# Second MoE by seven products: where its operands are prepared, and which 4 KB tile each step takes

## The chip, the cores and the metric

The kernel runs on one core of a Trainium2 chip. The metric is the device time of one execution in microseconds (us). Its engines are named as the profile names them: PE (TensorE, matrix products), PEld (its weight loads), DVE (VectorE), ACT (ScalarE), POOL (GpSimd) and SP (SyncE, which here issues every DMA).

## What is computed

A softmax attention without a score matrix feeds a gated MoE and then a second MoE. All weights come as float64, and the result is float32.

```python
def _attn_ref(q, k, v):                    # each (8, 8, 576, 64)
    q_s = softmax of q over the last axis
    k_s = softmax of k over the 576 positions
    kv = np.einsum('bhsd,bhse->bhde', k_s, v)
    return np.einsum('bhsd,bhde->bhse', q_s, kv)

def _moe_ref(x, w_gate, w_val, w_out):     # x (4608, 512), d_ff 1536
    g = x @ w_gate
    silu = g * (1.0 / (1.0 + np.exp(-g)))
    return silu * (x @ w_val) @ w_out

def _moe2_ref(x, w_in, w_out):             # d_ff 2048
    h = x @ w_in
    g = np.where(h > 0.0, h, np.exp(np.minimum(h, 0.0)) - 1.0)
    return g @ w_out
```

(The two softmaxes are written out in the reference; here they are abridged.)

## The kernel before

The 4608 tokens are nine blocks of 512, numbered 0 to 8. Every matrix product is done three times with operands split into a high and a low part (high by high, high by low, low by high), so one product of two 128-wide operands is three PE instructions.

**First MoE, two passes.** `run_1` goes over the nine blocks twice: pass "a" with the first six chunks of d_ff (the attention of the next block is computed beside it, `side_1a`), pass "b" with the other six. A block of a pass is six chunks of three slots: slot 0 is the gate product and its silu on ACT (`silu_act`, L798 to L801), slot 1 the value product and silu's products on DVE (L805, L808, L811), slot 2 the product with `w_out` of the chunk before (`emit_B`) and the low half of the new `g` (L789). Each slot holds 12 matmuls, so a block has 216. The gate lies in one of two PSUM banks (`a0`, `a1`); PE may start the next gate only when L808 has read the last one. At a block's end four DVE adds (L845) form the block's result `ys`, which goes to DRAM.

**Weights.** `conv`, called in slots of both passes, turns float64 weights into the split form: a load into a `raw` tile (L142, L144), a scaling on ACT, three bit operations on DVE (L171 to L178), a split on ACT and POOL (L201, L202, L217 to L231), and a store to DRAM (`sd` for the second MoE's input weights, `wd` for its output weights).

**Operands of the second MoE.** It computes blocks in pairs by seven products (M1 to M7) of sums of quarter blocks. Its operands, `xd`, are made from `ys` by `prep_open` and `prep_step`: the first loads four tiles of one half (c = 0 or 1) of a pair into the tile `yr` (L935), the second makes one operand per call. That is a difference of quarters on DVE where one is wanted (L917), a copy on ACT that rounds to the high part (L959), one call later the low part on DVE (L949) and a store of 512 KB (L950). The operands go round three buffers of the staging tile `xst`, so the copy of the fourth waits until the store of the first has landed. `side_b` decides when: in blocks 2 to 7 of pass b one half each, opened in slot 3 and stepped from slot 6 on; in block 8 both halves of the last pair (blocks 6 and 7), two steps per slot. Block 8 has no partner; its operands are made in `x_one`, in the second MoE (L910, L917).

**Second MoE.** `run_2` goes over four pairs and the single block 8 with the first half of d_ff (half 0), then over them in reverse order with the other half (half 1). One unit is four steps (two for the single block) of `step`: the seven products, four exponential units (`elu_act`, `elu_stt`, `elu_max`, `elu_hi`, `elu_lo`) on ACT and DVE, and between them, as `mid`, the products with `w_out2` of the step before (`emit_D`, 24 matmuls per step and block). A unit's last step goes through `after`: the loads of the next unit's operands are issued (`x_big`, `x_small`: one tile of M1 and M6, six of M7, M5 and M2, one of M3 and M4), then comes the last `emit_D` of the first block with its evacuation (`evac`, L1085 to L1088), then `rest` (the fourth exponential unit), then the sums of the second block, whose last part is carried into the next unit's first step.

**Order and tiles.** The order on every engine is the order in which the code is written (`manual_schedule`), and all DMAs stand in one queue, SP's. Tiles of 4 KB a partition come from three pools, `w` (19), `raw` (3) and `g` (3), by `slot4`, which takes the first pool in a given order that has room.

## Time and profile before

| | |
|---|---|
| time, median of 3 runs | 1827.46 us (1827.08 to 1829.01) |
| time of the profiled execution | 1828.21 us |
| its span, first to last instruction | 1826.3 us |
| mean granted TensorE clock, share of full speed | 0.974 |
| busy: PE, PEld, DVE, ACT, POOL | 1713.7, 1399.4, 1147.1, 873.2, 164.3 us |
| moved by DMA | 317.32 MB, mean 174 GB/s |

The span is what the profile sees; 1.9 us of the execution lie around it. Busy time is the union of an engine's instructions; a matmul's end is modelled, so neighbours overlap a little. Line numbers (L...) are those of the kernel before. In a row on a stretch stand its start and end, its length, the busy time of PE, PEld, DVE, ACT and POOL (with the instructions in brackets), the granted clock as a share of full speed, the busy share of the DMA engines and GB/s.

### The profile page before, as it was taken

Reading aid. Unit: us, or ns where it says so; the run is one execution under the profiler, and the core shown is the slowest. Engines: PE = TensorE matmul, PEld = TensorE weight load, DVE = VectorE, ACT = ScalarE, POOL = GpSimd, SP = SyncE. Lnnn points to the kernel's source line nnn. Section 1 sums busy time; section 2 is a strip of 40 time slices with the busy share of each in tenths; the row PEclk is TensorE's granted clock in tenths of the full one; section 3 lists DMA queues with packets and bytes.
Section 4 is the critical chain, followed back from the end, with each engine's and each line's share of the span. In section 5 each row is a group of like instructions: output and inputs, shape, how many; then the busy total and the mean of one; then the engine's idle time right before and its main releaser. Section 6 shows DMA issues by size and latency. Waiting matters only on the chain.

```text
span 1826.3 us, 21717 instructions
## 1 busy us (share of the span) xinstructions
PE 1713.7 (94%) x8264; PEld 1399.4 (77%) x8264; DVE 1147.1 (63%) x1763; ACT 873.2 (48%) x1534; POOL 164.3 (9%) x140
## 2 busy tenths in 40 slices
PE   6799999999999979899997699999979889999999
PEld 4677888888788867677885578888869768888887
DVE  7867777775686666677553474746564447475574
ACT  5555444444464545455442364645453436354453
POOL 3620000000031434111000000000000000000000
PEclk9899999999999999999998799999989989999999
DMA  9374576543554786777557833314014713341511
GB/s 277 111 205 131 147 185 160 169 127 120 177 189 143 281 311 243 269 292 286 208 196 295 321 133 149 139 70 184 24 46 177 305 48 129 125 185 69 208 46 70
DMA packets 148360, 317.32 MB, mean 174 GB/s; under 512 B 46240, under 2 KB 97440, under 8 KB 134944
## 3 DMA queue, kind: packets, MB, share of 16 engines
q1 hardware_dynamic: 148256, 315.93, 50.1%
q8 instruction: 65, 1.06, 0.2%
q14 instruction: 39, 0.32, 0.1%
HBM read 200.54 MB, written 115.35 MB: 173 GB/s over the span
## 4 chain that ended last, share of the span: by engine, by line
PE 78%; DVE 8%; DMA 7%; ACT 5%; issue 1%; POOL 1%; SPq 1%; DVEq 0%; ACTq 0%; POOLq 0%
PE p L997 17%; PE y L753 11%; PE y L751 11%; PE y L752 10%; PE a L770 9%; PE a L771 9%; PE a L774 9%; DMA xd<-xst 3%; DMA yr<-ys 2%; PE t L431 1%; PE t L590 1%; DVE u L1121 1%; ACT th L1010 1%; ACT e L1011 1%; DVE g L1045 1%
## 5 line engine op out<-in xcount | busy, mean ns | idle before, releaser
L770 PE MATMUL a<-x,w 128*128 128x512 f32 x856 | 343.4, 401 | 57.6 <-DVE th L808 57.4
L771 PE MATMUL a<-x,w 128*128 128x512 f32 x856 | 338.5, 395 | 0.7 <-POOL x L599 0.7
L751 PE MATMUL y<-w,g 128*128 128x512 f32 x576 | 227.7, 395 | 20.8 <-ACT g L1036 11.5
L770 PEld LDWEIGHTS a<-x,w 128*128 128x128 f32 x856 | 163.9, 191 | 103.2 <-DVE th L808 56.8
L774 PE MATMUL a<-x,w 128*128 128x512 f32 x856 | 232.0, 393 | 0.0
L753 PE MATMUL y<-w,g 128*128 128x512 f32 x576 | 227.7, 395 | 0.8
L752 PE MATMUL y<-w,g 128*128 128x512 f32 x576 | 226.8, 394 | 0.0
L1121 DVE TENSOR_TENSOR u<-u,p 128x512 f32<-128x512 f32 x180 | 123.4, 686 | 139.7 <-PE p L997 131.8
L771 PEld LDWEIGHTS a<-x,w 128*128 128x128 f32 x856 | 164.1, 192 | 34.5 <-POOL x L599 1.2
L774 PEld LDWEIGHTS a<-x,w 128*128 128x128 f32 x856 | 163.1, 191 | 34.6
L997 PE MATMUL p<-xp,s 128*128 128x512 f32 x768 | 182.3, 391 | 3.9 <-DVE u L1121 3.9
L783 ACT ACTIVATE g<-th 128x512 fp32r<-128x512 f32 x108 | 68.3, 632 | 241.6 <-DVE th L811 241.6
L805 DVE SCALAR_TENSOR_TENSOR th<-th,e 128x512 f32<-128x512 f32 x108 | 77.5, 717 | 159.7 <-ACT th L801 159.7
L752 PE MATMUL y<-g,w 128*128 128x512 f32 x432 | 169.7, 393 | 2.4 <-POOL g L789 2.4
L753 PE MATMUL y<-g,w 128*128 128x512 f32 x432 | 170.0, 394 | 1.5 <-POOL w L202 1.5
L997 PEld LDWEIGHTS p<-xp,s 128*128 128x128 f32 x768 | 144.6, 189 | 34.8 <-DVE u L1121 4.8
L751 PE MATMUL y<-g,w 128*128 128x512 f32 x432 | 170.1, 394 | 1.2 <-ACT w L201 1.2
L1016 DVE SCALAR_TENSOR_TENSOR th<-e,th 128x512 f32<-128x512 f32 x144 | 99.3, 690 | 100.7 <-ACT e L1011 99.1
L997 PE MATMUL p<-xs,s 128*128 128x512 f32 (+1 forms) x720 | 154.6, 369 | 0.4 <-DVE u L1121 0.4
L751 PEld LDWEIGHTS y<-w,g 128*128 128x128 f32 x576 | 110.0, 191 | 44.8 <-ACT g L1036 12.4
L997 PEld LDWEIGHTS p<-xs,s 128*128 128x128 f32 x720 | 126.4, 189 | 23.4 <-DVE u L1121 0.6
L798 ACT ACTIVATE e<-a 128x512 f32<-128x512 f32 x107 | 63.8, 597 | 168.0 <-PE a L774 167.9
(179 smaller groups left out, 2532.0 us busy)
## 6 DMA issues: line engine op xcount, KB each, us to landing
xp<-xd SPq DMA_DIRECT2D x32, 1024.0 KB, 7.8
xd<-xst SPq DMA_DIRECT2D x56, 512.0 KB, 5.7
xs<-xd SPq DMA_DIRECT2D x48, 512.0 KB, 10.8
xs<-x SPq DMA_DIRECT2D x9, 2048.0 KB, 7.0
x<-xs SPq DMA_DIRECT2D x36, 512.0 KB, 8.0
sd<-s SPq DMA_DIRECT2D x8, 1792.0 KB, 6.8
s<-sd SPq DMA_DIRECT2D x8, 1792.0 KB, 14.0
raw<-in_moe_w_out SPq DMA_DIRECT2D x26, 512.0 KB, 4.9
```

Of the source, the lines that this page charges most:

```text
L751: nc.tensor.matmul(out=ps, lhsT=wh, rhs=xh, start=first, stop=False)
L752: nc.tensor.matmul(out=ps, lhsT=wh, rhs=xl, start=False, stop=False)
L753: nc.tensor.matmul(out=ps, lhsT=wl, rhs=xh, start=False, stop=last)
L770: nc.tensor.matmul(out=ps, lhsT=wh, rhs=x[:, c, 0, :], start=(c == 0), stop=False)
L771: nc.tensor.matmul(out=ps, lhsT=wh, rhs=x[:, c, 1, :], start=False, stop=False)
L774: nc.tensor.matmul(out=ps, lhsT=wl, rhs=x[:, c, 0, :], start=False, stop=(c == KD - 1))
L783: nc.scalar.activation(out=gt[:, 0, :], in_=src, func=ACTF.Copy)
L798: nc.scalar.activation(out=e, in_=gate, func=ACTF.Relu, scale=-1.0)
L805: nc.vector.scalar_tensor_tensor(out=t, in0=t, scalar=1.0, in1=e, op0=ALU.add, op1=ALU.mult)
L997: nc.tensor.matmul(out=out_, lhsT=w, rhs=x, start=first and (q, c, k) == (0, 0, 0), stop=(c, k) == (1, 2), skip_group_check=True,)
L1016: nc.vector.scalar_tensor_tensor(out=t, in0=e, scalar=1.0, in1=t, op0=ALU.add, op1=ALU.mult)
L1121: nc.vector.tensor_tensor(o, a, b, op=ALU.add)
```

## The change

The first two pieces of the diff give the kernel charge of the 4 KB tiles: 25 of them in one pool, each with its own name, a list of vacant ones, and `slot4` takes the one that has been vacant longest among the kinds it is given. `g`, `raw` and `w` tiles of the first MoE go through it too. In `side_b`, blocks 5, 6 and 7 of pass b now hold six openings, one every nine slots, for both halves of pairs 0, 1 and 2; blocks 2 to 4 and block 8 hold none. The halves of pair 3 and the single block are prepared by `prep_window`, behind `rest` of the pairs 0, 1 and 2 in half 0; `x_one` only loads. Two of four loads of input weights and four of eight of output weights for half 0 move from the end of block 8 into the first two steps of `run_2`. The single block's last sums are carried into the next unit, as a pair's were.

```diff
-    CAP = {"w": NW1, "raw": NRAW, "g": 3}
-    used = dict.fromkeys(CAP, 0)
+    KINDS = ("w",) * NW1 + ("raw",) * NRAW + ("g",) * 3
+    vacant = list(range(len(KINDS)))
+    ANY = ("w", "raw", "g")
...
+    def slot4(kinds, shape, name, dtype=F32R):
+        for n in vacant:
+            if KINDS[n] in kinds:
+                vacant.remove(n)
+                return n, wp.tile(shape, dtype, tag=f"m{n}", name=name)
         raise AssertionError(name)
 
-    def drop(tag):
-        used[tag] -= 1
+    def drop(n):
+        vacant.append(n)
...
+    PREP0 = 5
...
+    def prep_now(m, c, ops, outs):
+        lo = []
+
+        def finish():
+            op, src, d = lo.pop()
+            nc.vector.tensor_tensor(d[1], src, d[0].bitcast(FP32), op=ALU.subtract)
             for n in range(2):
+                nc.sync.dma_start(out=xd[m][PROD[op]][:, c, n], in_=d[n].bitcast(FP32))
+
+        for op, src, pre in ops:
+            d = outs.pop(0)
+            outs.append(d)
+            pre()
+            nc.scalar.activation(out=d[0], in_=src, func=ACTF.Copy)
+            if lo:
+                finish()
+            lo.append((op, src, d))
+        finish()
+
+    def prep_window(n):
+        m, single = (NB // 2 - 1, False) if n < 2 else (NB // 2, True)
+        at = [slot4(ANY, [128, 2, TB], "yr") for _ in range(3)]
+        r = [t[:, e].bitcast(FP32) for _, t in at[:2] for e in range(2)]
...
+        for t, (b, c) in zip(r, src):
+            nc.sync.dma_start(out=t, in_=ys[b][:, c])
...
+        if single:
+            outs = [(t[:, 0:256], t[:, 256:]) for t in (at[2][1][:, 0], at[2][1][:, 1], st[:, 0], st[:, 1], *cd)]
+            for c in range(2):
+                t = cg()
+                prep_now(m, c, prep_ops(
+                    r[2 * c][:, 0:256], r[2 * c][:, 256:], r[2 * c + 1][:, 0:256],
+                    r[2 * c + 1][:, 256:], t[:, 0:256], t[:, 256:],
+                ), outs)
+        else:
+            outs = [(at[2][1][:, 0], at[2][1][:, 1]), (st[:, 0], st[:, 1]), cd[0:2], cd[2:4]]
+            prep_now(m, n, prep_ops(*r, cg(), cg()), outs)
+        for t, _ in at:
+            drop(t)
...
     def side_b(i, ff, s):
...
+        n = (i - PREP0) * 3 * HALF + 3 * ff + s
+        if n < 0 or n > 6 * 9:
+            return
+        if n % 9 != 1:
+            prep_step()
+        if n % 9 == 0 and n < 6 * 9:
+            assert not prep
+            prep_open(n // 18, n // 9 % 2)
...
         if s == 2 and ff >= 1:
-            while len(wtag) < F2 // 2 and used["w"] < NW1:
-                load_p(len(wtag))
+            while len(wtag) < 4 and room(("w",)):
+                load_p(len(wtag), ("w",))
         if (ff, s) == (HALF - 1, 2):
-            assert not prep
             x_big(units[0], X_LAST)
-            load_s(2)
-            load_s(3)
...
             for k, q in enumerate(gs[:-1]):
+                if n == 0 and k < 2:
+                    load_s(2 + k)
+                    load_p(4 + 2 * k)
+                    load_p(5 + 2 * k)
...
                 if len(u) == 1:
                     rest()
-                dd(u[0], k, drop_w=turn)()
-                if len(u) == 2:
+                    carry.append(lambda a=(half, u[0], fs[k], turn): emit_D(*a))
+                else:
+                    dd(u[0], k)()
                     rest()
+                    if n < 3:
+                        prep_window(n)
```

Three places in the built order show what moves. The first is SP's queue in block 5 of pass b, from the load of the next block's input on. Before:

```order
L1252 DMA x<-xs_148 128x1024 x4
L950 DMA xd_185<-xst 128x1024
L204 DMA wd_119<-w 128x1024
L144 DMA raw<-in_moe_w_out 128x512
L950 DMA xd_188<-xst 128x1024
L853 DMA ev<-yp_156 128x2048
L950 DMA xd_186<-xst 128x1024
L950 DMA xd_189<-xst 128x1024
L204 DMA wd_120<-w 128x1024
L950 DMA xd_187<-xst 128x1024
L950 DMA xd_191<-xst 128x1024
```

and with the change (`yr<-ys` are the loads of the next half):

```order
L1277 DMA x<-xs_142 128x1024 x4
L984 DMA xd_176<-xst 128x1024
L984 DMA xd_174<-xst 128x1024
L208 DMA wd_113<-w 128x1024
L147 DMA raw<-in_moe_w_out 128x512
L984 DMA xd_178<-xst 128x1024
L862 DMA ev<-yp_150 128x2048
L984 DMA xd_177<-xst 128x1024
L969 DMA yr<-ys_154 128x512
L969 DMA yr<-ys_155 128x512
L969 DMA yr<-ys_154 128x512
L969 DMA yr<-ys_155 128x512
```

Before, seven stores `xd<-xst` of one half stand in this block; with the change the seven of one half are followed at once by the loads and stores of the next, in the same queue as the weight traffic (`wd`, `raw`), the next block's input (`x<-xs`) and the partial sums (`ev<-yp`).

The second is DVE where the first pair of the second MoE hands over to the second (`ev<-y` is the evacuation, `u<-u,p` the next step's first sums). Before:

```order
L1087 COPY ev<-y_8499 128x512
L1087 COPY ev<-y_8501 128x512
L1016 SCALAR_TENSOR_TENSOR th<-e,th 128x512
L1022 TENSOR_TENSOR th<-th,u 128x512
L1045 TENSOR_TENSOR g_8861<-th,g_8861 128x512
L1121 TENSOR_TENSOR u<-u,p_8947 128x512
L1121 TENSOR_TENSOR u<-u,p_8954 128x512
```

and with the change:

```order
L1073 TENSOR_TENSOR g_8800<-th,g_8800 128x512
L951 TENSOR_TENSOR u<-yr 128x512
L951 TENSOR_TENSOR u<-yr,u 128x512
L910 TENSOR_TENSOR yr<-yr 128x512
L910 TENSOR_TENSOR st<-u,st 128x512
L910 TENSOR_TENSOR xo<-yr,xo 128x512
L951 TENSOR_TENSOR yr<-yr,u 128x512
L910 TENSOR_TENSOR xo<-u,xo 128x512
L910 TENSOR_TENSOR yr<-yr 128x512
L951 TENSOR_TENSOR yr<-yr 128x512
L910 TENSOR_TENSOR st<-yr,st 128x512
L910 TENSOR_TENSOR xo<-yr,xo 128x512
```

Between the low part of `rest` (the last row of the `g` kind) and the next unit's sums stand eleven operations on what `ys` gives, and ACT has seven copies at the same place.

The third is PE where the single block passes from half 0 to half 1 (`p<-xa,s` and `p<-xs,s` are products, `y<-w,g` the sums with the output weights). Before, the products of half 1 follow the last sum:

```order
L751 MATMUL y_11086<-w_8215,g_11165 128x512
L752 MATMUL y_11086<-w_8215,g_11165 128x512
L753 MATMUL y_11086<-w_8215,g_11165 128x512
L997 MATMUL p_11252<-xa,s 128x256 x12
L997 MATMUL p_11265<-xa,s 128x256 x12
L997 MATMUL p_11278<-xa,s 128x256 x12
L997 MATMUL p_11296<-xa,s 128x256 x12
L997 MATMUL p_11252<-xs,s 128x256 x12
```

With the change the first five of these products stand ahead of the second half of the sums:

```order
L759 MATMUL y_11156<-w_8113,g_11004 128x512
L760 MATMUL y_11156<-w_8113,g_11004 128x512
L761 MATMUL y_11156<-w_8113,g_11004 128x512
L1025 MATMUL p_11260<-xa,s 128x256 x12
L1025 MATMUL p_11273<-xa,s 128x256 x12
L1025 MATMUL p_11286<-xa,s 128x256 x12
L1025 MATMUL p_11304<-xa,s 128x256 x12
L1025 MATMUL p_11260<-xs,s 128x256 x12
L759 MATMUL y_11153<-w_8272,g_11220 128x512
L760 MATMUL y_11153<-w_8272,g_11220 128x512
L761 MATMUL y_11153<-w_8272,g_11220 128x512
```

The 48 matmuls of the carried sums now follow the fifth product instead of standing ahead of the first. The same move is made where the single block hands over to pair 3 in half 1.

## Rows read from the trace of the kernel before

**Rows 1.** The page: TensorE's busy time, and its granted clock in 40 slices.
```profile
PE 1713.7 (94%) x8264; PEld 1399.4 (77%) x8264; DVE 1147.1 (63%) x1763; ACT 873.2 (48%) x1534; POOL 164.3 (9%) x140
PEclk9899999999999999999998799999989989999999
```

**Rows 2.** Waits of PE: who waited for whom, us in all, times, longest.
```profile
PE a L770 <- DVE th L808: 57.4, 11, 20.8
PE y L751 <- ACT g L1036: 11.5, 2, 5.8
PE y L751 <- DVE ev L1087: 9.3, 1, 9.3
```

**Rows 3.** Stretches of pass b, cut where L845 starts.
```profile
591.80:640.83 49.03, 49.03 (x218) 40.58 (x217) 32.22 (x47) 25.23 (x45) 23.07 (x21) 1.00 0.73 263
640.83:703.87 63.04, 52.30 (x217) 42.12 (x216) 40.55 (x59) 29.10 (x52) 22.14 (x21) 0.92 0.77 279
703.87:765.51 61.64, 51.55 (x216) 41.50 (x215) 39.99 (x58) 28.90 (x52) 15.90 (x13) 0.94 0.76 282
765.51:817.20 51.69, 49.26 (x217) 40.46 (x217) 37.61 (x58) 26.80 (x49) 8.29 (x6) 1.00 0.82 295
817.20:868.35 51.15, 49.26 (x217) 40.47 (x217) 38.64 (x58) 26.23 (x48) 7.79 (x6) 1.00 0.71 267
917.31:966.27 48.96, 48.96 (x217) 40.54 (x217) 25.48 (x41) 20.31 (x37) 0.00 (x0) 1.00 0.50 183
966.27:1048.79 82.52, 55.49 (x219) 44.45 (x219) 32.81 (x52) 23.98 (x43) 0.00 (x0) 0.81 0.88 334
```

**Rows 4.** Line L845: shortest, median, longest ns; first and last start.
```profile
L845 DVE TENSOR_TENSOR ev<-y,ev x36: 681/681/692, 591.8 to 1050.8; 128x512 f32<-128x512 f32 x36
```

**Rows 5.** Chain of waits, blocks 2 and 8: start us, us, what.
```profile
648.96 8.17 DMA yr<-ys
669.46 11.73 DMA xd<-xst
...
988.62 16.36 DMA xd<-xst
1013.36 10.92 DMA yr<-ys
```

**Rows 6.** Stretches of the second MoE, cut where a unit's first product starts.
```profile
1041.10:1122.04 80.94, 79.50 (x350) 65.17 (x348) 50.74 (x77) 42.32 (x71) 0.00 (x0) 1.00 0.48 189
1122.04:1204.04 82.00, 81.90 (x362) 67.51 (x360) 47.61 (x72) 42.67 (x72) 0.00 (x0) 1.00 0.30 116
1286.04:1380.22 94.18, 84.81 (x361) 69.36 (x360) 55.36 (x94) 47.50 (x86) 0.00 (x0) 0.95 0.09 34
1380.22:1489.46 109.24, 95.00 (x553) 84.14 (x552) 50.87 (x91) 44.73 (x88) 0.00 (x0) 0.94 0.51 202
1489.46:1570.50 81.04, 78.35 (x337) 64.07 (x336) 48.45 (x74) 40.47 (x68) 0.00 (x0) 0.98 0.38 143
```

**Rows 7.** Stretches: products with 256 columns; all DMA engines busy.
```profile
1392.90:1405.80 12.90, 12.90 (x109) 12.90 (x108) 8.82 (x17) 8.29 (x17) 0.00 (x0) 1.00 0.80 310
1090.00:1108.00 18.00, 17.91 (x80) 14.47 (x79) 12.35 (x19) 11.02 (x20) 0.00 (x0) 1.00 1.00 398
```

**Rows 8.** Timeline of ACT, blocks 7 and 5: start, us; idle in brackets.
```profile
946.35 0.64 ACT L959 ACTIVATE xst<-yr 128x512 fp32r<-128x512 f32 x1 [2.60 <-DMA xd<-xst]
848.72 0.63 ACT L959 ACTIVATE xst<-yr 128x512 fp32r<-128x512 f32 x1 [1.94 <-DMA xd<-xst]
```

**Rows 9.** The first pairs' turn, timeline of SP and ACT.
```profile
1088.66 3.57 SPq L872 DMA_DIRECT2D xs<-xd  x6
1106.54 0.32 SPq L1088 DMA_DIRECT2D y<-ev  x1
1123.60 0.60 ACT L1140 ACTIVATE u<-p 128x512 f32<-128x512 f32 x1 [13.11 <-PE p L997]
```

**Rows 10.** The four stores of the output's last block, as DMA issues.
```profile
out<-ev SPq DMA_DIRECT2D x4, 256.0 KB, 2.4
```

More of the change, by code (lines that the diff above doesn't have):

```diff
@@ L97, with room @@
         chunks.append((("p", f), wsrc_rows(w_out2, f), False))
-    CAP = {"w": NW1, "raw": NRAW, "g": 3}
-    used = dict.fromkeys(CAP, 0)
-    def slot4(order, shape, name):
-        for tag in order:
-            if used[tag] < CAP[tag]:
-                used[tag] += 1
-                pool = {"w": wp, "raw": raw_p, "g": g_p}[tag]
-                return tag, pool.tile(shape, F32R, tag=tag, name=name, bufs=CAP[tag])
+    KINDS = ("w",) * NW1 + ("raw",) * NRAW + ("g",) * 3
+    vacant = list(range(len(KINDS)))
+    ANY = ("w", "raw", "g")
+    def room(kinds):
+        return sum(KINDS[n] in kinds for n in vacant)
+    def slot4(kinds, shape, name, dtype=F32R):
[3 more added lines that the diff above has]
+                return n, wp.tile(shape, dtype, tag=f"m{n}", name=name)
         raise AssertionError(name)
-    def drop(tag):
-        used[tag] -= 1
+    def drop(n):
+        vacant.append(n)
     sd = [dr.tile([128, 7, 2, 256], FP32, name=f"sd{g}") for g in range(2 * NG2)]
@@ L139, in conv_load @@
         _, src, cols = chunks[n]
-        t = early.pop(n) if n in early else raw_p.tile([128, 512], I64, tag="raw", name="raw")
+        t = early.pop(n) if n in early else None
+        if t is None:
+            rslot[n], t = slot4(("raw",), [128, 512], "raw", I64)
         if cols:
@@ L194, in conv_split @@
             return
-        if used["w"] >= NW1:
+        if not room(("w",)):
             return
-        used["w"] += 1
-        w = wp.tile([128, 2, 512], F32R, tag="w", name="w", bufs=NW1)
+        at, w = slot4(("w",), [128, 2, 512], "w")
         stage["split"] += 1
@@ L533 @@
     xd = [
-        {op: dr.tile([128, 2, 2, TB], FP32, name=f"xd{t}{op}") for op in range(7)}
-        for t in range(NB // 2)
+        {
+            op: dr.tile([128, 2, 2, TB if t < NB // 2 else TB // 2], FP32, name=f"xd{t}{op}")
+            for op in range(7)
+        }
+        for t in range(NB // 2 + 1)
     ]
@@ L876, in x_small @@
                 o[op] = [t[:, c] for c in range(2)]
+                nc.sync.dma_start(out=t.bitcast(FP32), in_=xd[u[0] // 2][PROD[op]])
     def x_big(u, ops):
@@ new lines, in prep_window @@
+    def prep_window(n):
+        m, single = (NB // 2 - 1, False) if n < 2 else (NB // 2, True)
+        at = [slot4(ANY, [128, 2, TB], "yr") for _ in range(3)]
+        r = [t[:, e].bitcast(FP32) for _, t in at[:2] for e in range(2)]
+        src = [(2 * m, n), (2 * m + 1, n), (2 * m, n + 2), (2 * m + 1, n + 2)]
+        if single:
+            src = [(2 * m, 0), (2 * m, 2), (2 * m, 1), (2 * m, 3)]
+        for t, (b, c) in zip(r, src):
+            nc.sync.dma_start(out=t, in_=ys[b][:, c])
+        st = cv_p.tile([128, 4, 256], F32R, tag="st", name="st", bufs=1)
+        st = st.rearrange("p (a b) n -> p a (b n)", a=2)
+        cd = [cv_p.tile([128, TB], F32R, tag="cd", name="xo", bufs=NCD) for _ in range(4)]
+        if single:
+            outs = [(t[:, 0:256], t[:, 256:]) for t in (at[2][1][:, 0], at[2][1][:, 1], st[:, 0], st[:, 1], *cd)]
[10 more added lines that the diff above has]
+            drop(t)
@@ L1027, in g_tile @@
         if key not in G2:
-            G2[key] = slot4(("g", "w", "raw"), [128, 2, TB], "g2")
+            G2[key] = slot4(ANY, [128, 2, TB], "g2")
         return G2[key][1]
@@ L1421, in run_2 @@
                     x_big(nxt, X_HEAD)
-                    x_small(nxt, X_MID, ("raw", "w", "g"))
+                    x_small(nxt, X_MID, ANY)
             k = len(gs) - 1
@@ L1439, in after @@
                             x_big(nxt, X_HEAD)
-                            x_small(nxt, X_MID, ("raw", "w", "g"))
+                            x_small(nxt, X_MID, ANY)
                     if len(nxt) == 2:
```

63 lines of the change are left out of this document (16 added, 47 removed).

## Prediction

> **What bounds the kernel now.** PE is busy for 1713.7 of 1826.3 us [rows 1], so only its idle time, and what it does at the lower of its two clock levels, can be saved. The granted clock's digits are 8 in the second slice, 8 and 7 in the 22nd and 23rd, 8 in the 30th and the 33rd, and 9 elsewhere [rows 1]; a slice is 45.7 us. The list of PE's waits names the releasers [rows 2]: 57.4 us in eleven waits for L808, which frees the gate's PSUM bank, 11.5 for the high part of an exponential unit (L1036), 9.3 for an evacuation (L1087). Those that begin in the first 110 us are not touched.
>
> Next I read pass b by block. I cut it where the sums at a block's end (L845, [rows 4]) start, once per block. An undisturbed block takes 48.96 us, with or without seven operands in it (917 to 966; block 1 has none and takes 49.03) [rows 3]. That is 216 matmuls, 0.2267 us each. Blocks 2 to 5 take 14.1, 12.7, 2.7 and 2.2 us more. The last stretch holds block 8 and runs up to the sums of block 8, ahead of which stand five products (30 matmuls) instead of two projections (24): 48.96 + 6 x 0.2267 = 50.3, so its 82.52 us hold 32.2 us of loss. The loss is idle time plus the matmuls after it at half the clock (mean 0.92, 0.94 and 0.81 there, 1.00 elsewhere [rows 3]).
>
> Who is late there shows the chain of waits [rows 5]: DVE waits for loads of `ys` (8.17 us, 10.92 us), and ACT waits to write a staging buffer until a store has landed (11.73 us, 16.36 us). ACT and DVE work in written order, so silu stands behind these waits, L808 comes late, and PE has no bank.
>
> In the second MoE a pair of 360 matmuls takes 82.00 us, 0.2278 each [rows 6]. The stretch of pair 3 takes 94.18 because `x_one` stands ahead of the evacuation: 12.2 us. In the single block's stretch the 256-column products cost 12.90 / 108 = 0.12 us each [rows 7]: 336 x 0.12 + 216 x 0.2278 = 89.5, so 109.24 holds 19.7 us of loss. The next unit has 336 matmuls (no carried sums), 76.5 us, and takes 81.04: 4.5. The first unit has 348, 79.3, and takes 80.94: 1.7.
>
> **The change, part by part.**
>
> *Blocks 2 to 4* lose their operands: no loads of `ys`, no stores, and 11 DVE and 7 ACT operations fewer each. The weight conversion stays. That block 1 has the same conversion at 263 GB/s and loses nothing [rows 3] says that the 14.1 + 12.7 + 2.7 = **29.5 us** go. Next late there would be the gate's own chain, which fits in 48.96.
>
> *Block 8* loses both halves of pair 3, and nothing on DVE or ACT waits for a DMA there until its sums. The loads for the first unit stay in it; PE needs them only at its end. **32.2 us** go. The moved loads cost nothing: the third and fourth input-weight loads are now issued at the start of steps 0 and 1 and are wanted in steps 2 and 3, about 30 us later.
>
> *Pair 3's stretch*: `x_one` issues seven loads and computes nothing. The evacuation follows the sums as in other pairs: **12.2 us** go.
>
> *The single block*: the carried sums put five products (5.5 to 7 us) between a step's end and the sums that wait for its fourth exponential unit; the wait on L1036 was about 5.8 us each time [rows 2]. It is also shortened, since the tile for the high part is now the longest vacant and not one that PE still reads. The step that had no sums between its products now has 48 matmuls there, so the next step's banks are free in time. **19.7 + 4.5 us** go; I leave nothing, and keep 0 to 4 us for the range.
>
> *Blocks 5 to 7* take six halves in 54 slots, twice as dense. DVE and ACT have room: in the undisturbed block with seven operands they are busy 25.5 and 20.3 of 48.96 us, block 5 has 38.6 and 26.2 [rows 3], and eleven DVE operations of 0.69 us make 7.6 more, 46 of 49 in block 5. The queue is the question. Block 5 moves 267 GB/s x 51.15 us = 13.7 MB; seven stores of 0.524 and four loads of 0.262 MB more make 18.4, over 48.96 us 375 GB/s. The highest rate held over a long stretch is 398, with all DMA engines busy [rows 7]. So it fits as a mean, not in its bursts: between the sixth and the eleventh slot of block 5 stand two `wd`, two `raw`, five `xd`, the next input (2.1 MB), the partial sums and the next `ys` (1.05 each), 8.9 MB or 22 us of transfer in 14 us of slots. The store of the fourth operand lies behind some 3.1 MB, 8 us, plus 1.7 (a 256 KB store lands in 2.4 us [rows 10], 0.7 of it transfer), while its buffer is wanted again some 6 us after. How much lateness PE bears is in rows: the copy of the sixth operand began 29.0 us after the cut in block 7, where PE lost nothing, and 31.5 after it in block 5, where it lost 2.2 [rows 8, 3]. So 4 us of lateness cost PE about 3 to 4; the first operand of the next half waits likewise for its `ys`, another 2, and the denser DVE half a microsecond at the block's start: **6.5 us** instead of 2.2. Blocks 6 and 7 have 194 or less + 96 GB/s and no weight work; there the same store waits behind 2.1 MB, 5.3 + 1.7 + its own 1.3 us, and just makes it: 0. Bounds: 0, and block 2's 14.1 for each half in block 5, 28.
>
> The Trainium skill, "DMA: Bandwidth & Descriptors" (Specifications), puts the HBM limit of one core at about 358 GB/s. By that block 5 could not take less than 51.4 us, the queue would drain a tenth slower, and the 6.5 would be about 9, the forecast 1738. The trace's 398 GB/s over 18 us, much of it reads of `xd` from DRAM, does not agree, and I keep to the row.
>
> *The windows* behind `rest` of pairs 0 to 2. ACT is idle there for 13.11 us until the next unit's first copy at 1123.60 [rows 9], DVE as long. A pair's window is 11 DVE operations (7.6 us), 7 ACT copies, 4 loads and 14 stores of 256 KB. Its loads stand in SP's queue behind the evacuation's store, issued at 1106.54, and behind the next operands. Of these six tiles two are now ones that the mid sums (24 matmuls after 1094.7) free, so most go out at 1097 to 1104 instead of 1088.66 to 1092 [rows 9]. From 1097.4 on 7.3 MB have to pass: 18.4 us at 398 GB/s, 1115.9, landed at 1117.5. Then 7.6 us of DVE and about 1 us for reuse of the four output buffers: 1126. The next copy is then 2.5 us late, and PE asks for its bank after four products, 24 x 0.2278 = 5.5 us after the unit's start at 1122.04, at 1127.5. So nothing is lost, with 1 us to spare. The third window (single block: 22 DVE operations on 256 columns, 28 stores that SP issues at about half a microsecond each) ends about 1.5 us after that point. **1.5 us** for the three; bounds 0 and, as in `x_one`, 12.2 each.
>
> **Sum.** 1828.2 - 29.5 - 32.2 - 12.2 - 24.2 - 2.2 + 6.5 + 1.5 = 1735.9 for the profiled execution, which stands 0.75 us above the median of the runs: **1735 us**, 5.1% less.
>
> **The rivals.**
> - *Block 5 becomes a new block 2*: its first half, or both, lose what bursts cost in blocks 2 and 3. For: the burst is of their size (18.4 MB in the block against 279 x 63.04 = 17.6). Against: no 1.8 MB `sd` stores. 14 to 28 instead of 6.5: 1743 to 1757.
> - *The windows push the next unit*: should each end 4 to 12 us too late (loads landing after 1121), PE idles and restarts at half clock; 12 to 36 us, 1747 to 1771. For: 1 us of margin. Against: nothing else moves then.
> - *The change does not reach blocks 2 to 4*, because weight traffic and not the operands made the stalls: 29.5 us stay, 1764. Against: block 1.
> - *Slower*: stores take everywhere what they took in block 2 (11.73 us). Then six halves lose 14.1 each (84.6 instead of 6.5) and three windows 12.2 each (36.6 instead of 1.5): 1735 + 78 + 35 = 1848. It decides from about 92 us of new loss on, some 10 us for every half and window. Against: in blocks 6 and 7 DMA is half idle [rows 3].
>
> **How the numbers follow.** Forecast 0.68 (1728 to 1743), block 5 0.14, windows 0.09, blocks 2 to 4 0.05, slower 0.04. The range 1728 to 1755 leaves out most of the last three and a little of the second, about 0.18. A measurement tells 0.2% (3.7 us) from no change; all cases but the last are far beyond: faster 0.95, within 0.01, slower 0.04.
>
> **What would show it.** In the changed kernel's stretches, cut as here: blocks 2 to 4 at 49.0, block 5 near 55, blocks 6 and 7 at 49 to 50, the last near 50.3; units of 82 us, the single block near 78.6 and the one after it near 87.5 (48 matmuls, 10.9 us, change sides); no dip of the granted clock after 110 us. PE's wait on L808 would be left in block 5 alone. Waits of ACT for `xd` stores in blocks 6 and 7, or of PE at a unit's fifth product behind a window, would show my two small terms wrong; a first cause that I do not see would be a wait at a place with neither operands nor windows.

## The result, and the profile after

The changed kernel takes 1741.12 us, median of four runs (1739.46 to 1745.43), against 1827.27 (1827.08 to 1829.01) for the kernel before: ratio 0.953, with a 95% interval from 0.9512 to 0.9549. The forecast was 1735, the range 1728 to 1755. The profiled execution took 1745.43 us (span 1743.7); it is the slowest of the four, 4.3 us above their median.

The page of the changed kernel, TensorE's busy time and its granted clock in 40 slices (compare [rows 1]):

```profile
PE 1692.9 (97%) x8264; PEld 1386.3 (80%) x8264; DVE 1144.9 (66%) x1763; ACT 872.6 (50%) x1534; POOL 164.5 (9%) x140
...
PEclk9899999999999999999999999999999999999999
```

The digits of 7 and 8 in the second half of the span are gone. Here are the stretches of pass b for blocks 2 to 8, cut where the sums at a block's end start (L854 in this kernel's numbering; compare [rows 3]; the columns are the same):

```profile
639.52:688.49 48.97, 48.97 (x218) 40.56 (x217) 32.69 (x48) 25.22 (x45) 22.58 (x21) 1.00 0.73 263
688.49:736.94 48.45, 48.45 (x215) 40.16 (x214) 31.66 (x48) 25.13 (x45) 16.35 (x13) 1.00 0.72 261
736.94:785.89 48.95, 48.95 (x217) 40.55 (x217) 30.89 (x47) 23.06 (x42) 7.74 (x6) 1.00 0.62 221
785.89:844.94 59.05, 53.47 (x224) 43.60 (x224) 45.30 (x70) 30.04 (x55) 7.78 (x6) 0.94 0.83 311
844.94:895.88 50.94, 47.81 (x211) 39.30 (x210) 32.57 (x51) 24.79 (x45) 1.30 (x1) 1.00 0.79 281
895.88:946.77 50.89, 49.27 (x217) 40.48 (x217) 32.47 (x51) 24.04 (x44) 0.00 (x0) 1.00 0.71 260
946.77:996.22 49.45, 49.45 (x219) 40.96 (x219) 18.95 (x30) 16.27 (x29) 0.00 (x0) 1.00 0.85 341
```

Blocks 2 to 4 run at 48.5 to 49.0, and the last stretch takes 49.45 instead of 82.52. Blocks 5 to 7 take 59.05, 50.94 and 50.89, 160.88 together, which is 14.0 more than 3 x 48.96. (A cut can shift by a few matmuls: block 5 holds 224 here and block 6 has 211, so the three are best read together.)

The stretches of the second MoE from the second unit on, cut where a unit's first product starts (compare [rows 6]); the fourth is the single block, both halves:

```profile
1069.44:1153.96 84.52, 82.51 (x362) 67.35 (x360) 54.42 (x84) 46.74 (x80) 0.00 (x0) 1.00 0.46 168
1153.96:1238.64 84.68, 82.52 (x361) 67.36 (x360) 56.71 (x90) 47.78 (x83) 0.00 (x0) 1.00 0.47 169
1238.64:1321.33 82.69, 82.21 (x362) 67.44 (x361) 52.73 (x87) 45.39 (x80) 0.00 (x0) 1.00 0.31 111
1321.33:1399.80 78.47, 78.47 (x505) 71.85 (x504) 46.80 (x84) 42.97 (x86) 0.00 (x0) 1.00 0.69 272
1399.80:1487.22 87.42, 87.33 (x385) 72.03 (x384) 52.52 (x80) 41.39 (x71) 0.00 (x0) 1.00 0.37 134
```

The three units behind a window take 84.52, 84.68 and 82.69 instead of 82.00, 5.9 us together. The single block takes 78.47 for 109.24, and the unit behind it 87.42 with 48 matmuls more than before. PE's waits between 110 us and the end (who waited for whom: us in all, times, longest; compare [rows 2]):

```profile
PE a L778 <- DVE th L816: 10.3, 3, 5.6
PE p L1025 <- ACT u L1168: 4.1, 3, 1.9
PE p L1025 <- DVE u L1149: 1.5, 2, 1.3
```

The first row is blocks 5 to 7, one wait in each (5.6, 3.1 and 1.6 us). The second is the three windows. The third holds the 1.3 us at the first unit's start, which was there before the change too.

**Blocks 5 to 7.** In ACT's timeline (start, us, instruction; idle time before it and its releaser in brackets) the seventh copy of each first half has waited for the store of the fourth operand:

```profile
812.95 0.63 ACT L993 ACTIVATE xst<-yr 128x512 fp32r<-128x512 f32 x1 [5.89 <-DMA xd<-xst]
...
868.09 0.63 ACT L993 ACTIVATE xst<-yr 128x512 fp32r<-128x512 f32 x1 [7.00 <-DMA xd<-xst]
...
918.96 0.63 ACT L993 ACTIVATE xst<-yr 128x512 fp32r<-128x512 f32 x1 [5.49 <-DMA xd<-xst]
```

(In block 5 the sixth copy had already waited 2.1 us for the store of the third.) silu of the next slot stands behind this copy on ACT, and PE's gate behind silu. Why the store was late is seen in SP's timeline in block 5, where the next block's input (four loads, L1277) and the stores of the fourth and fifth operand (L984) are issued:

```profile
799.97 3.26 SPq L1277 DMA_DIRECT2D x<-xs  x4
803.33 0.94 SPq L984 DMA_DIRECT2D xd<-xst  x2
```

SP needs 3.26 us to issue the four loads, the store goes out behind them at 803.33, and its 0.52 MB queue behind their 2.1 MB; it landed 9.5 us later. In blocks 6 and 7 the same store took 10.5 and 10.0 us. In the chain of waits (start, us, what):

```profile
803.33 9.54 DMA xd<-xst
...
857.51 10.50 DMA xd<-xst
...
908.87 10.01 DMA xd<-xst
```

In block 5 a second loss follows. After the 5.6 us of idle time PE's first matmuls run at the lower clock level:

```profile
817.09:823.09 6.00, 6.00 (x15) 4.70 (x15) 3.37 (x5) 2.46 (x5) 1.29 (x1) 0.51 1.02 390
```

Fourteen matmuls begin in these 6.0 us (the fifteenth in the row begins at their end); undisturbed they take 14 x 0.2267 = 3.2, so 2.8 us are lost here beside the 5.6. Block 5's whole loss is 8.4 us: 59.05 less the 50.66 that the same 224 matmuls take in a run below without a wait (e12).

**The windows.** The first window's loads, in the chain of waits (start, us, what):

```profile
1054.95 12.90 DMA yr<-ys
```

It landed at 1067.9, the last of the four at 1069.1, and the next unit started at 1069.44. DVE's eleven operations ran from 1067.95 to 1077.47, and PE waited 1.8 us for the unit's first copy, which stands behind the window's seven copies on ACT.

### The profile page after: what moved, and what is told of

Read it like the earlier page. It is cut to its first block, busy times and chain, and to the rows that moved or that the text cites. A ratio compares the mean times of both kernels' runs of the same rounds, so it can differ in the third digit from the quotient of the medians.

```text
span 1743.7 us, 21796 instructions
## 1 busy us (share of the span) xinstructions
PE 1692.9 (97%) x8264; PEld 1386.3 (80%) x8264; DVE 1144.9 (66%) x1763; ACT 872.6 (50%) x1534; POOL 164.5 (9%) x140
## 4 chain that ended last, share of the span: by engine, by line
PE 81%; DVE 6%; DMA 6%; ACT 4%; issue 1%; POOL 1%; SPq 1%; DVEq 0%; ACTq 0%; POOLq 0%
PE p L1025 17%; PE y L761 11%; PE a L778 10%; PE y L759 10%; PE y L760 10%; PE a L779 10%; PE a L782 10%; DMA yr<-ys 2%; DMA xd<-xst 2%; PE t L436 1%; PE t L598 1%; DVE u L1149 1%; ACT th L1038 1%; DVE g L1073 1%; ACT e L1037 1%
## 5 line engine op out<-in xcount | busy, mean ns | idle before, releaser
L761 PE MATMUL y<-w,g 128*128 128x512 f32 x576 | 225.1, 391 | 0.7
L760 PE MATMUL y<-w,g 128*128 128x512 f32 x576 | 224.3, 389 | 0.0
L759 PE MATMUL y<-w,g 128*128 128x512 f32 x576 | 224.2, 389 | 0.0
L778 PEld LDWEIGHTS a<-x,w 128*128 128x128 f32 x856 | 162.2, 189 | 59.1 <-issue 12.5
L779 PEld LDWEIGHTS a<-x,w 128*128 128x128 f32 x856 | 162.3, 190 | 34.0 <-POOL x L607 1.1
L782 PEld LDWEIGHTS a<-x,w 128*128 128x128 f32 x856 | 161.4, 189 | 33.8
L1037 ACT ACTIVATE e<-u 128x512 f32<-128x512 f32 x108 | 67.7, 627 | 146.7 <-DVE u L1149 146.7
```

What stands on the lines that cost most here:

```text
L759: nc.tensor.matmul(out=ps, lhsT=wh, rhs=xh, start=first, stop=False)
L760: nc.tensor.matmul(out=ps, lhsT=wh, rhs=xl, start=False, stop=False)
L761: nc.tensor.matmul(out=ps, lhsT=wl, rhs=xh, start=False, stop=last)
L778: nc.tensor.matmul(out=ps, lhsT=wh, rhs=x[:, c, 0, :], start=(c == 0), stop=False)
L779: nc.tensor.matmul(out=ps, lhsT=wh, rhs=x[:, c, 1, :], start=False, stop=False)
L782: nc.tensor.matmul(out=ps, lhsT=wl, rhs=x[:, c, 0, :], start=False, stop=(c == KD - 1))
```

## The experiments

Each kernel is the changed one with the edit shown, where nothing else is said. Line numbers differ a little between them.

| run | edit | median, us | blocks 5 to 7 | units behind windows | single block and next unit |
|---|---|---|---|---|---|
| changed kernel | | 1741.1 | 160.9 | 251.9 | 165.9 |
| e1_six_buffers | six staging buffers | 1744.3 | 159.5 | 254.9 | 165.9 |
| e6_spread_x | input loads one a slot | 1745.1 | 158.7 | 252.5 | 165.9 |
| e8_loads_ahead | e1, and loads of `ys` 4 slots earlier | 1739.0 | 152.3 | 253.4 | 165.9 |
| e12_three_waits | e8, and own staging for `wd` | 1732.5 | 147.1 | 251.5 | 165.9 |
| e2_early_ys | windows' loads earlier | 1735.7 | 156.5 | 246.0 | 165.9 |
| e13_all | e12 and e2 | 1727.3 | 147.1 | 246.0 | 165.9 |
| e7_half_a_block | a half a block, blocks 2 to 7 | 1764.6 | 149.3 | 251.1 | 165.9 |
| e4_no_carry | no carry | 1753.3 | 156.6 | 251.5 | 175.0 |
| e5_newest_tile | newest tiles | 1769.2 | 156.5 | 251.1 | 184.0 |
| e11_newest_no_carry | both | 1781.3 | 157.6 | 251.0 | 194.3 |
| e14_handout_only | kernel before, with the hand-out | 1814.8 | | | 175.6 |
| e15_carry_only | kernel before, with the carry | 1809.7 | | | 171.1 |

The three columns on the right are of each run's profiled execution. Undisturbed, they would be 146.9, 246.0 and some 166. In the two runs with the newest tiles the units behind windows are long because of the tiles (each of the pairs' units is), not of the windows. The kernel before was measured again beside each group of runs, with medians of 1828.3 to 1829.3. Five profiles with the changed kernel's blocks 5 to 7 (the changed kernel's own, e2, e4, e5, e11) give 156.5 to 160.9 for them.

### What stalls blocks 5 to 7

**e1_six_buffers.** The operands go round six staging buffers instead of three:

```diff
-        s_ = w2_pool[0].tile([128, 7, 2, 256], F32R, tag="s1", name="xst")
...
+        for g in () if xst else (1, 2):
+            s_ = w2_pool[0].tile([128, 7, 2, 256], F32R, tag=f"s{g}", name="xst")
...
+            xst.extend(s_[:, k] for k in range(3))
```

> The changed kernel with one edit: the operands of blocks 5 to 7 go round six staging buffers instead of three (the second three lie in a weight tile that is vacant then). In the changed kernel blocks 5, 6 and 7, cut at the sums, take 59.05, 50.94 and 50.89 us, 160.9 together, 14.0 more than 3 x 48.96. Theory 1: all of it comes from the seventh copy of each first half, which waits 5.9, 7.0 and 5.5 us for the store of the fourth, queued behind the next block's input. Six buffers put the wait three operands further on, where that store has landed: the three blocks take 147 to 148 us, 13 to 14 us less, a median near 1728. Theory 2: the queue is full whatever the buffers (18.4 MB in block 5, and no stretch of 18 us of this kernel has moved more than 384 GB/s): block 5 keeps 52 to 54 us, because the next half's loads and the input come late instead, and only 6 to 10 us go, a median of 1731 to 1735.

Both theories failed: the time did not fall. No copy waited for a store any more, and yet block 5 took 60.87 us. Its stretch:

```profile
786.02:846.89 60.87, 53.42 (x223) 43.36 (x223) 44.24 (x69) 30.02 (x55) 7.75 (x6) 0.92 0.81 302
```

and DVE's timeline there, at the first operation of the next half:

```profile
823.71 0.69 DVE L951 TENSOR_TENSOR yr<-yr 128x512 f32<-128x512 f32 x1 [7.89 <-DMA yr<-ys]
```

7.89 us of waiting for the loads of `ys`: in the queue they stand behind the same burst. In the changed kernel the store's wait came first and had made PE late already, so this one showed only on ACT and DVE. Theory 2 had named the loads, but had priced them at 3 to 5 us.

**e6_spread_x.** The burst is taken apart, with three buffers as in the changed kernel:

```diff
-        for c in range(KD):
-            nc.sync.dma_start(out=x_t[blocks[n]][:, c].bitcast(FP32), in_=xs[blocks[n][1]][:, c])
+        todo.extend((blocks[n], c) for c in range(KD))
...
                         side_b(i, ff, s)
+                        load_c()
```

> The changed kernel with one edit: the four loads of the next block's input (0.52 MB each) are issued one a slot in slots 5 to 8 instead of all four behind slot 5; three staging buffers as in the changed kernel. Theory 1: the fourth operand's store was late because of the burst of 2.1 MB ahead of it. It then has one load ahead of it, lands some 4 us earlier, and the seventh copy begins 4 us earlier: blocks 6 and 7 lose nothing (49.0 each), block 5, whose queue holds weight traffic too, 0 to 3 us; 11 to 14 us less, a median near 1729. Theory 2: the amount in the queue decides, not its order: the seventh copies wait as before, or those of the sixth and of the next half instead, and the time stays within 4 us of 1741.

Theory 2: at 1745.1 us the time stays where it was. ACT's waits from 780 to 930 us show what moved; in the changed kernel the same two rows (from 785 to 930) were 7.0 us for the loads and 21.4 for the stores:

```profile
ACT xst L993 <- DMA yr<-ys: 18.9, 4, 6.9
...
ACT xst L993 <- DMA xd<-xst: 2.1, 2, 1.2
```

The input loads that no longer stand ahead of the fourth store now stand ahead of the next half's loads. As long as every buffer is this shallow, the order in the queue only chooses who waits.

**e8_loads_ahead.** Six buffers, and the loads of a half four slots earlier, into two tiles in turn:

```diff
+        if n % 9 == 5 and -9 < n < 5 * 9:
+            prep_load((n + 4) // 18, (n + 4) // 9 % 2)
```

> The changed kernel with two edits: six staging buffers, and the four loads of every half in blocks 5 to 7 issued four slots earlier, into one of two tiles in turn (the second is a weight tile that is vacant then). With six buffers alone the copies no longer waited for stores, but the next half's first operations waited up to 7.9 us for its loads, which stand in the same queue behind the same burst, and blocks 5 to 7 took 159.5 us, cut at the sums, against 160.9 and, of unchanged code in two other runs, 156.5. Theory 1: both waits are the latency of one queue, some 10 us behind the burst, and each goes when its transfer is asked for early enough: the three blocks take 147 to 149 us, a median of 1728 to 1731. Theory 2: block 5 asks for more than the queue carries (18.4 MB in 48.96 us is 375 GB/s; the busiest 20 us of it ran at 384, the whole block at 302 to 313): lateness piles up whatever stands early, block 5 keeps 53 to 56 us, and the median is 1733 to 1737.

Blocks 6 and 7 are whole, 211 and 217 matmuls at 0.225 us; block 5 is not:

```profile
787.78:843.58 55.80, 52.42 (x224) 42.60 (x224) 44.76 (x70) 30.07 (x55) 7.79 (x6) 0.97 0.88 328
843.58:891.09 47.51, 47.51 (x211) 39.38 (x210) 32.31 (x51) 24.62 (x45) 1.30 (x1) 1.00 0.84 301
891.09:940.05 48.96, 48.96 (x217) 40.55 (x217) 32.28 (x51) 24.09 (x44) 0.00 (x0) 1.00 0.70 258
```

In ACT's timeline in block 5:

```profile
819.95 0.63 ACT L205 ACTIVATE w<-cd 128x512 fp32r<-128x512 f32 x1 [5.22 <-DMA wd<-w]
```

So neither theory held for the whole (block 5 has Theory 2's length, but, as the next run shows, not for its reason): in block 5 there was a third wait, 5.22 us of ACT for the store of a converted output weight (`wd`), whose 4 KB tile is the only one that the first MoE leaves for it. PE waited 3.4 us behind it.

**e12_three_waits.** The converted weights get two staging places of their own as well:

```diff
+        if kind == "p" and spare:
...
+            w = spare.pop(0)
+            spare.append(w)
```

> The changed kernel with three edits: six staging buffers, the loads of each half four slots earlier, and, new, the converted output weights staged in two places of their own instead of the one first-MoE weight tile that is vacant. With the first two edits blocks 6 and 7 took 47.5 and 49.0 us and block 5 55.8: ACT waited 5.2 us there for the store of a converted weight that stands in the queue behind the same burst. Theory 1: that is the third wait of the same kind and the last: block 5 takes 49 to 51 us (its DVE has 45 us of work in 49), the three blocks 147 to 149, and the median is 1733 to 1736, 4 to 5 under the run with two edits. Theory 2: the queue in block 5 is behind for good, and a fourth wait (the raw weights, the partial sums, the next input) takes its place: block 5 keeps 53 us or more, a median of 1736 to 1739.

Theory 1 (the median is half a us below what it gave): no idle time of PE is left in the three blocks, and the clock stays at 1.00.

```profile
785.80:836.46 50.66, 50.66 (x224) 41.61 (x224) 43.95 (x69) 30.03 (x55) 7.78 (x6) 1.00 0.94 349
836.46:883.96 47.50, 47.50 (x211) 39.35 (x210) 32.31 (x51) 24.57 (x45) 1.30 (x1) 1.00 0.87 314
883.96:932.92 48.96, 48.96 (x217) 40.54 (x217) 32.28 (x52) 24.07 (x44) 0.00 (x0) 1.00 0.68 258
```

Block 5 moves its bytes at 349 GB/s without harm, with the DMA engines busy 0.94 of the time. So it was no lack of rate: three sets of one to three buffers (`xst`, `yr` and the tile for `wd`) each waited for a transfer that took 9 to 12 us behind a burst, one hiding behind the other. A converted weight's store goes out as two of half the size in this run; no run parts that from the second place.

### The windows

**e2_early_ys.** The tiles for `ys` are taken before the next unit's, and loaded between its small and its last operands:

```diff
+                    if n < 3:
+                        at = window_tiles()
                     for tag in X.pop(u)[1]:
                         drop(tag)
...
+                    if n < 3:
+                        window_loads(n, at)
                     if len(nxt) == 2:
                         x_big(nxt, X_LAST)
```

> The changed kernel with one edit: the four loads of a window are issued between the next unit's small and last operands, ahead of the evacuation's store, instead of behind rest. In the changed kernel they land 2.2 to 0.3 us ahead of the next unit's start, and the units behind the three windows take 84.5, 84.7 and 82.7 us instead of 82.0: 5.9 us together. Theory 1: the windows are late because their loads are: they will land some 5 to 10 us earlier, the work ends before the unit's fifth product asks, and the three units take 82.0 to 82.2, 5 to 6 us less in all, a median near 1735.5. Theory 2: the window's own length decides (eleven DVE operations that took 9.5 us, with waits of up to 1.1 us for its four output buffers to be stored), or the next unit's own operands, now 1 MB later in the queue, come late: less than 2 us go, or some us come on top, 1740 to 1745.

Theory 1, to the number: the three units take 82.0 each.

```profile
1066.42:1148.41 81.99, 81.90 (x362) 67.49 (x361) 54.70 (x83) 46.72 (x79) 0.00 (x0) 1.00 0.46 175
1148.41:1230.39 81.98, 81.89 (x361) 67.49 (x360) 55.75 (x94) 47.69 (x86) 0.00 (x0) 1.00 0.44 166
1230.39:1312.38 81.99, 81.90 (x361) 67.50 (x360) 47.66 (x72) 42.63 (x72) 0.00 (x0) 1.00 0.24 86
```

The first window's loads now land at 1049.0 to 1051.0, 15 us ahead of the unit, where 5 to 10 us earlier than before was expected; its work starts when `rest` ends, and all of it is done before the unit starts.

**e13_all.** Both repairs together:

> The same kernel with the windows' loads issued ahead of the evacuation's store as well. Alone, that edit made the units behind the three windows 82.0 us each and the median 5.4 us less. Theory 1: the two are independent: 5 to 7 us less than the run with three edits, a median of 1727 to 1730, no idle time of PE over 1 us behind 110 us but at the first unit's start. Theory 2: with block 5's stall gone another place sets the time, and the median stays above 1732.

1727.32 us (1724.97 to 1727.49), ratio to the kernel before 0.9443 (0.9429 to 0.9457): 13.8 us below the changed kernel's median, and every run of it below every run of the changed kernel. Theory 1: the two are independent. PE's waits from 110 to 1720 us:

```profile
PE p L1055 <- DVE u L1179: 1.3, 1, 1.3
PE a L790 <- POOL x L618: 0.7, 1, 0.7
```

What is left of idle time on PE lies in the first 110 us (the second row is a wait at that edge), but for the 1.3 us at the first unit's start.

### Whether the operands made the stalls of blocks 2 to 5

**e7_half_a_block.** `side_b` opens one half a block again, in blocks 2 to 7 (pair 3 stays in the windows):

```diff
-        n = (i - PREP0) * 3 * HALF + 3 * ff + s
+        m, c = divmod(i - 2, 2)
+        n = 3 * ff + s
+        if n == 3:
+            prep_open(m, c)
+        if n >= 6:
+            prep_step()
```

> The changed kernel with one part undone: the halves of pairs 0 to 2 lie in blocks 2 to 7 again, one a block, as before; pair 3 and the single block stay behind the pairs' sums, and the tiles are handed out as changed. Theory 1 (the prediction's): the operands made the stalls of blocks 2 to 5, so these take about 63, 62, 52 and 51 us again, blocks 6 and 7 49 each, block 8 stays near 49.5: 31.7 us come back and 10 to 14 go, a median of 1757 to 1763. Theory 2: the stalls came from how the first MoE's 4 KB tiles were taken from three pools, which stays changed here, or from pair 3's operands late in the pass: blocks 2 and 3 take 49 to 54, and the median is 1728 to 1741.

Theory 1: the stalls come back, block by block, within some 2 us of [rows 3], and 23.5 us with them (the median, 1764.6, is 1.6 us above what was given).

```profile
640.29:702.70 62.41, 52.31 (x216) 42.10 (x215) 40.34 (x59) 29.10 (x52) 22.08 (x21) 0.92 0.78 282
702.70:765.01 62.31, 51.45 (x216) 41.48 (x216) 39.84 (x59) 28.86 (x52) 15.88 (x13) 0.95 0.76 278
765.01:818.71 53.70, 50.88 (x217) 41.60 (x217) 37.63 (x59) 26.77 (x49) 7.75 (x6) 0.97 0.78 284
818.71:870.06 51.35, 49.29 (x217) 40.47 (x217) 38.65 (x58) 26.21 (x48) 7.76 (x6) 1.00 0.71 266
```

### What freed the single block

Five runs cross the two parts that could have done it, the carry and the hand-out of tiles. The stretches are the single block and the unit behind it.

**e4_no_carry.**

```diff
-                    carry.append(lambda a=(half, u[0], fs[k], turn): emit_D(*a))
+                    dd(u[0], k, drop_w=turn)()
```

> The changed kernel with one part undone: the single block's last sums stand again ahead of the next unit's products. Theory 1 (the prediction's): the carry removes PE's waits for the fourth exponential unit; without it some 17 to 24 us come back in the single block's two halves and the unit behind them (78.47 and 87.42 us in the changed kernel, 165.9 together; 109.24 + 81.04 = 190.3 before), a median of 1758 to 1765. Theory 2: the tile for the high part, which is now the one vacant longest, is what mattered, and the carry little: 3 to 10 us come back, 1744 to 1751.

Nearer to Theory 2: 9.1 us come back in these stretches, within its 3 to 10, and 12.1 in the median, between the two ranges.

```profile
1319.14:1414.67 95.53, 91.72 (x553) 82.10 (x552) 50.69 (x91) 44.13 (x88) 0.00 (x0) 0.98 0.59 232
1414.67:1494.15 79.48, 76.79 (x338) 62.91 (x336) 48.27 (x74) 40.45 (x68) 0.00 (x0) 1.00 0.38 139
```

**e5_newest_tile.**

```diff
-        for n in vacant:
+        for n in vacant[::-1] if name == "g2" else list(vacant):
```

> The changed kernel with one part turned round: the exponential units' tiles are those vacant for the shortest time, the rest as changed. Without the carry the single block's halves and the unit behind them took 175.0 us, 9.1 more than with it (165.9), and 190.3 in the kernel before: so about 15 us of the 24.2 that went are not the carry's. Theory 1: they are the hand-out's, but with the carry in place its five products (5.5 to 7 us) hide such a wait: 0 to 3 us come back, a median of 1741 to 1744. Theory 2: the waits for a tile that PE still reads come back beside the carry, here and in the pairs' steps: 5 to 15 us or more, a median of 1746 to 1756. Theory 3: neither; the 15 us went with the computations of x_one, and nothing changes.

Theory 2, and more than it said: 28 us in the median. The first row is a pair's unit, which loses too; then come the single block and the unit behind it:

```profile
1066.56:1150.26 83.70, 82.56 (x361) 67.27 (x360) 54.73 (x83) 47.13 (x79) 0.00 (x0) 1.00 0.47 170
1317.66:1403.34 85.68, 80.79 (x506) 73.40 (x504) 43.30 (x76) 37.97 (x74) 0.00 (x0) 0.98 0.60 239
1403.34:1501.69 98.35, 91.30 (x385) 73.73 (x384) 55.57 (x88) 46.99 (x82) 0.00 (x0) 0.97 0.35 134
```

ACT's wait, in the last two stretches, for PE to finish reading the tile that it is about to write:

```profile
ACT g L1064 <- PE y L761: 37.9, 8, 9.3
```

In the changed kernel no such wait appears there.

**e11_newest_no_carry**, both turned back:

> The changed kernel with both turned back: no carry behind the single block, and the exponential units' tiles the newest vacant ones. It stands beside the run without the carry alone (1753.3 median; single block and next unit 175.0 us) and the one with the newest tiles alone. If the hand-out is worth the 15 us that the carry isn't, the single block and the unit behind it take 185 to 192 us here, as the 190.3 before, and the median is 1763 to 1771; if the 15 us went with the computations of x_one, 174 to 177 us and a median within 3 us of 1753.

113.18 and 81.11, 194.3 us in the two stretches, a little over what was given, and 1781 instead of 1763 to 1771, since the pairs' units lose as well. The carry is worth 10.3 us here and 9.1 with the oldest tiles.

But newest-first is not what the kernel before did (its pairs ran at 82.0 us), so the last two runs put each part alone into the kernel before.

**e14_handout_only** has the first two pieces of the diff and no other; **e15_carry_only** has the carry and no other.

> The kernel before with one part of the change alone: the 4 KB tiles are handed out by the kernel, the longest vacant first; operands, windows and the single block's sums as before. The single block and the unit behind it took 190.3 us before, 175.0 in the changed kernel without the carry, and 194.3 there with the newest tiles and no carry. If the hand-out alone is worth the difference, they take 174 to 177 us here, and the median is 1811 to 1816; if the 15 us are not the hand-out's but came with the move of the single block's operands into a window, 188 to 191 us and 1824 to 1830.

> The kernel before with the other part alone: the single block's last sums are carried into the next unit; tiles from the three pools as before. By the prediction's step the carry removes all 24.2 us of loss: single block and next unit take 166 to 169 us, a median of 1803 to 1807. If it hides only what its five products cover, as the two runs with the newest tiles say (184.0 with, 194.3 without), some 9 to 12 us go: 178 to 182 us, a median of 1815 to 1819.

The two stretches with the hand-out alone:

```profile
1379.64:1474.19 94.55, 90.47 (x554) 80.65 (x552) 50.68 (x91) 44.26 (x88) 0.00 (x0) 1.00 0.59 234
1474.19:1555.22 81.03, 78.36 (x337) 64.08 (x336) 48.44 (x74) 40.43 (x68) 0.00 (x0) 0.98 0.39 143
```

With the carry alone:

```profile
1379.46:1460.37 80.91, 78.74 (x506) 71.90 (x505) 44.14 (x78) 40.62 (x79) 0.00 (x0) 1.00 0.67 265
1460.37:1550.57 90.20, 87.62 (x385) 71.92 (x384) 55.30 (x86) 44.30 (x77) 0.00 (x0) 1.00 0.36 136
```

and PE's waits in these two stretches:

```profile
PE p L997 <- ACT u L1140: 4.7, 2, 2.5
```

ACT's waits for PE to finish reading a tile, in the two stretches, first of the kernel before, then with the carry alone; with the hand-out alone there is none:

```profile
ACT g L1036 <- PE y L753: 10.9, 5, 3.2
...
ACT g L1036 <- PE y L753: 13.8, 7, 3.2
```

The hand-out alone takes the 190.3 us to 175.6, 14.7 less, as expected if it was worth the difference. The carry alone takes them to 171.1, 19.2 less, which lies between its two expectations: 4.7 us of PE's waits stay, for a copy of ACT that stands behind writes into tiles still being read. Together they bring 24.4, not 33.9. Each hides a part of what the other removes. As whole kernels the two runs are 0.8% and 1.0% faster than the kernel before, small but outside their intervals (ratios 0.9902 to 0.9945 and 0.9866 to 0.9929).

## Why the prediction was right, point by point

The sum was made against the profiled executions: 1735.9 forecast, 1745.4 measured, 9.5 more. (Between the medians it is 6.1; of five profiles this one has the longest blocks 5 to 7.) The losses that were to go went; the two small terms for new losses were both put too low. Term by term:

- **Blocks 2 to 4** (29.5 us to go, 49.0 a block): 48.97, 48.45 and 48.95. Right in place, size and cause: with the halves back in blocks 2 to 5 the losses came back (e7). The rival that blamed the weight traffic is out.
- **Block 8** (32.2; 50.3 to remain): 49.45. Right in size. The hand-out alone and the carry alone leave the stretch at 82.6 and 81.6 (e14, e15), so neither did it alone; no run parts the operands of pair 3 from the six weight loads that left this stretch with them, and that it was the operands rests on the chain of waits [rows 5].
- **Pair 3's stretch** (12.2): 82.69, of which 0.7 is the third window's; 81.99 in e2. Right; with the hand-out or the carry alone it keeps 94.1 and 93.7.
- **Single block** (19.7 + 4.5; 78.6 and 87.5 to remain): 78.47 and 87.42. The sum is right, the reason only in part. The step let the carry remove it all and called the tile's choice a help; alone the carry leaves 5.2 us, and the hand-out alone removes 14.7 (e15, e14).
- **Blocks 5 to 7** (6.5 us lost, in block 5 alone): 14.0 in this profile, 9.6 to 10.7 in four others. This is the larger mis-sized term. The mechanism and place were right: the seventh copy waits for the fourth operand's store, behind the burst. Three sizes were not. First, the buffer was taken to be wanted 6 us after the store; in block 5 it was wanted 3.7 after (803.33 to 812.95 - 5.89; 3.6 and 4.6 in blocks 6 and 7), because SP issues the store only after the four loads, which takes 3.26 us: the step counted their transfer and not their issue. Second, for blocks 6 and 7 the store's latency was put at 5.3 + 1.7 + 1.3 = 8.3 us; it was 10.5 and 10.0, and so PE lost 3.1 and 1.6 us where the step had nothing. Third, the matmuls at the lower clock level after the wait in block 5 cost 2.8 us, which the 6.5 did not hold. The 2 us put down for the late loads of `ys` did not show on PE, though the wait was there, hidden behind the store's; taking the store's wait away uncovered 7.9 us of it (e1).
- **The windows** (1.5, all of it in the third): 2.5, 2.7 and 0.7, 5.9 together. The failed step is the landing of the loads: 4.5 us ahead of the unit by the working, 2.2 to 0.3 measured. The working let 7.3 MB run at 398 GB/s from the first of the next operands' loads on, 20.1 us to the landing; it took 24.3, from that load's issue at 1044.77 to 1069.1, and the other five loads of its kind went out only from 1047.48 on. 1048 to 1066 us ran at 354 GB/s, with only 203 to 229 from 1046 to 1052. The 1 us of margin named there as the argument for the rival was not there. That the late loads were the cause is shown by e2.
- **The rest** of the difference: 1.3 us less ahead of block 1's sums, 0.9 in the last stretch, 0.5 in blocks 2 to 4. With 7.5 and 4.4 us more for the two small terms that makes 9.2 of the 9.5.

The signs named in advance for the two small terms being wrong both came: waits of ACT for `xd` stores in blocks 6 and 7, and waits of PE behind the windows. A dip of the granted clock after 110 us, which was not expected, came in block 5.

The prediction kept to its row against the HBM limit of some 358 GB/s in the Trainium skill's "DMA: Bandwidth & Descriptors" (Specifications). That page's section on bandwidth gives the figure as a core's part when both cores of a pair stream; this program has one. The changed kernel moved 384 GB/s from 800 to 820 us, which agrees with that reading. With its waits removed block 5 asked for 349 only, so its shortest time was never set by either figure.

**The rivals.** Block 5 as a new block 2 (14 to 28 us): it lost 8.4, 5.6 idle and 2.8 at the lower clock level. The windows pushing the next unit by 4 to 12 us each: the right place, at 0.7 to 2.7. Stores that take 11.7 us everywhere: the fourth store of each first half took 9.5 to 10.5, the median of all 42 is 3.3 on the changed kernel's page, and nothing like 10 us was lost per half.

## What to carry to other kernels

When a wait for a transfer in a shared queue is removed, look for the next transfer behind the same burst before pricing the gain: here three waits (store, load, weight store) stood one behind the other, and the first repair gained nothing, the first two together 2 us, all three 8.6. Count a burst's issue time on its queue beside its bytes, and ask for loads ahead of what they don't depend on. Hand out the scratch tile that has been vacant longest; here the newest was often still being read.

## What the runs showed of the hardware

- A 0.52 MB store that lands 2.6 us after its issue on a quiet queue took 9.3 to 10.5 us behind four loads of the same size, though these carry 2.1 MB only; each of the four costs SP 0.4 to 1.5 us to issue.
- TensorE's granted clock fell to the lower of its two levels at the 5.6 us of idle time in block 5 of the changed kernel, and at 3.4 us in e8 (0.97 in that stretch); after 3.1 us in block 6 it stayed at 1.00. The length of the wait does not decide it alone: at the first window of e8 1.8 us of idle time was enough (0.56 from 1070.1 to 1074.0), while in the changed kernel the waits of 1.8 and 1.9 us behind the first two windows left it at 1.00. So a stall of 2 to 3 us may or may not be paid for a second time, in matmuls at half speed.
- Blocks 5 to 7 of one and the same code took 156.5 to 160.9 us in five profiles, so such a stall is not the same in each execution; what makes the difference was not looked into. Why the queue ran at 203 to 229 GB/s from 1046 to 1052 us with the DMA engines busy about three quarters of the time stays open.
